# Softmax moved into the next unit's step and the last projections reordered, in a decode layer with attention and MLP on one core

## The chip, the cores and the metric

The kernel runs on one core of a Trainium2 chip. The core has a matrix engine (TensorE, PE in the profile, with its weight loads as PEld), a vector engine (VectorE, DVE), a scalar engine (ScalarE, ACT), GpSimd (POOL), and a sync engine (SP) whose queue issues nearly all transfers here. The 16 DMA engines of the core carry the transfers from device memory (HBM) to the on-chip memory. Each engine runs its own list of instructions in order and waits on semaphores for the others. The metric is the device time of one execution in microseconds; before and after are compared by the median of several executions.

## What is computed

Two branches of a transformer layer work on the same normalized input of two tokens (one per batch entry) and are added to the input: attention of 32 query heads over the last 2048 keys of a cache with 16 key heads, and an MLP with a squared ReLU.

```python
def _A_ref(x, k_cache, v_cache, wq, wo):     # B=2, D=576, Hq=32, Hkv=16, Dh=128
    W = min(4096, max(256, Sk // 4))          # Sk=8192, so W=2048
    q = (x @ wq) per head
    k, v = the last W rows of the caches, each key head used by two query heads
    scores = einsum("bhqd,bhkd->bhqk", q, k) * Dh ** -0.5
    o = einsum("bhqk,bhkd->bhqd", softmax(scores), v)
    return o @ wo
def _B_ref(x, w1, b1, w2, b2):               # F=4608
    h = x @ w1 + b1
    r = where(h > 0, h, 0)
    return (r * r) @ w2 + b2
return x + _A_ref(xn, ...) + _B_ref(xn, ...)  # xn = layernorm(x)
```

All arrays are bfloat16. With two rows of input, nearly all the bytes are caches and weights: 53.6 MB are read in one execution.

## The kernel before

The work on the caches is cut into 8 **units** (`NU`): unit `u` holds four key heads of one batch entry, 2048 KB of keys (`k_u`) and 2048 KB of values (`v_u`). Each is one transfer into a buffer of `kvpool`, which has six. The SP queue holds 25 loads in one fixed order, which runs `k0 wq k1 v0 w1 k2 v1 k3 v2 k4 v3 k5 v4 k6 v5 wo0 k7 v6 v7 wo1`, and then w2 in five pieces: `w2_0`, `w2_1`, `w2_2` (1296 KB each) and `w2_3` in two (1008 and 288 KB). A load that reuses a buffer waits in the SP queue until the last reader of that buffer is done, and the loads behind it wait too. `wo0` and `wo1` share one buffer.

One **step** (`step(u)`) does the key side of unit `u`. `transposes(u, g)`, for g = 0 to 7, turns the keys four 128x128 blocks at a time on PE into a PSUM tile `kT_ps` (three buffers), and copies the tile to SBUF, on ACT for even g and on DVE for odd g. `scores(u, w)`, for the two halves w, multiplies by the queries into `sc_ps`; each half needs the four copies of its half. In between go the value products of an earlier unit: `pv(u-2, i)`, i = 0 to 3, four matmuls each, into `pv_ps`. `pv_mix` then gathers the four parts of `pv_ps` on DVE (four instructions, three of them `mix`, the last into `acc`). `pv_out` brings one unit's `acc` to its place by a matmul into `sm`; for every fourth unit it also divides and rearranges on DVE into `ws`, which is the input of the output projection.

`softmax(u)` stands behind `scores(u, 1)`: the maximum of each row (`mx`, DVE), an offset (`m2`, shown as `m`), the maximum across partitions on GpSimd (`gmax`), two small DVE instructions (`gs`, `nb`), the exponential on ACT (`pr`, with its row sums), and a transpose on DVE (`pT`), which the value products of this unit need.

The order on PE is fixed by program order (`tc.keep_in_program_order` in `pe_mm` and `pe_tr`). On DVE and ACT only the four instructions of `pv_mix` are fixed among themselves; for the rest a scheduler of the language picks the order.

Ahead of the steps come `q_all` (query projection, which needs `wq`), and between step 1 and step 2 the hidden layer of the MLP: `mlp_h_start`, `mlp_h_all`, `mlp_h_end` (need `w1`). `mlp_h_end` copies the hidden rows to SBUF (`hrow`) and turns them into columns by 9 matmuls in fp32 with a selection matrix `sel_h`, which also adds the two partial sums (`hT_ps`).

At the end of the program stand, for unit numbers 4 to 7: step 6, the `sm` product of unit 4, all value products of unit 5, `wo_acc(0)` (32 matmuls of the first half of the output projection, into `out_ps`), the `sm` product of unit 5, step 7 without value products, the value products of units 6 and 7 with their `sm` products, `wo_acc(1)`, then `mlp_o` with `w2_0`, `w2_1` and `w2_2` (18 matmuls each, into the same `out_ps`). `out_ps` is copied to `part` by two DVE copies, `mlp_tail` multiplies with `w2_3` into `tail_ps` (28 matmuls for the first piece and 8 for the second, with the products that add `part` in between), and `fin_sb` leaves for the output.

Of the kernel before, what the change touches and what calls it, by code (L numbers as in the profile page):

```python
# [8 lines left out]
F32 = mybir.dt.float32  # L9
# [7 lines left out]
def kernel(  # L17
# [65 lines left out]
    def pe_mm(out, **kw):  # L83
        return tc.keep_in_program_order(nc.tensor.matmul(out, **kw))  # L84
# [3 lines left out]

    x2d = A_x.rearrange("b s d -> (b s) d")
# [51 lines left out]
    warm = const.tile([B, 114], F32, name="warm")  # L141
# [77 lines left out]
    sel_h = const.tile([P, NG4, B], F32, name="sel_h")  # L219
    for g in range(0, NG4, 2):  # L220
        q = (g + 2) % NG4
        idv = ident_f[:].rearrange("p (g s) -> p g s", s=32)
        nc.gpsimd.tensor_tensor(out=sel_h[:, g:g + 2, :], in0=idv[:, g:g + 2, 0:B], in1=idv[:, q:q + 2, B:2 * B],
                                op=ALU.add)
# [50 lines left out]
    def transposes(u, g):  # L275
        k_sb = k_tiles[u]
        w, gw = divmod(g, GW)
        if gw == 0:
            kT_tiles[(u, w)] = ktpool.tile([P, NT, P, 2], BF16, tag="kT_sb", name=f"kT_{u}_{w}")
        kT = kT_tiles[(u, w)]  # L280
        kT_ps = psum.tile([P, PG, P], F32, tag="kT", bufs=3, name=f"kT_ps_{u}_{g}")
        for i in range(PG):
            q = g * PG + i
            pe_tr(out=kT_ps[:, i, :], in_=k_sb[:, 2 * q * Dh:2 * (q + 1) * Dh].bitcast(F32),
                                identity=ident_f[:])
        src = kT_ps[:].rearrange("p i s -> p (i s)").bitcast(BF16)
        dst = kT[:, gw * PG:(gw + 1) * PG, :, :].rearrange("p i s e -> p (i s e)")
        if g % 2 == 0:
            nc.scalar.copy(out=dst, in_=src)  # L289
        else:  # L290
            nc.vector.tensor_copy(out=dst, in_=src)  # L291
# [16 lines left out]
    def softmax(u):  # L308
        sc_ps = sc_tiles.pop(u)[:].rearrange("p t s -> p (t s)")
        mx = work.tile([P, 1], F32, tag="mx", name=f"mx_{u}")  # L310
        nc.vector.tensor_reduce(out=mx[:], in_=sc_ps, axis=AX.X, op=ALU.max)  # L311
        m2 = work.tile([P, NC], F32, tag="m2", name=f"m2_{u}")
        nc.vector.tensor_scalar(out=m2[:], in0=offm[:], scalar1=mx[:, 0:1], scalar2=None, op0=ALU.add)  # L313
        gmax = work.tile([P, NC], F32, tag="gmax", name=f"gmax_{u}")
        nc.gpsimd.partition_all_reduce(gmax[:], m2[:], channels=P, reduce_op=ReduceOp.max)  # L315
        gs = work.tile([P, NC], F32, tag="gs", name=f"gs_{u}")
        nc.vector.tensor_tensor(out=gs[:], in0=gmax[:], in1=own_s[:], op=ALU.mult)
        nb = work.tile([P, 1], F32, tag="nb", name=f"nb_{u}")
        nc.vector.tensor_reduce(out=nb[:], in_=gs[:], axis=AX.X, op=ALU.add)  # L319
        pr = work.tile([P, NT * 32], BF16, tag="pr", name=f"pr_{u}")  # L320
        acc = keep.tile([P, Dh + 1], F32, tag="acc", bufs=4, name=f"acc_{u}")
        nc.scalar.activation(out=pr[:], in_=sc_ps, func=ACT.Exp, bias=nb[:], scale=scale, accum_out=acc[:, Dh:Dh + 1])  # L322
        pT = keep.tile([P, NT, 32], BF16, tag="pT", name=f"pT_{u}")
        nc.vector.transpose(out=pT[:].rearrange("p t m -> p (t m)"), in_=pr[:])  # L324
        pT_tiles[u], acc_tiles[u] = pT, acc
# [35 lines left out]
    def pv_out(u):  # L361
# [8 lines left out]
        if u % (2 * B) == 2 * B - 1:  # L370
            ri = work.tile([P, B], F32, tag="ri", name=f"ri_{t}")
            nc.vector.reciprocal(out=ri[:], in_=sm[:, :, Dh])
# [38 lines left out]
    def mlp_h_end():  # L411
# [10 lines left out]
        hv = hs[:].rearrange("p r (g b) -> p g r b", b=B)  # L422
        nc.vector.tensor_tensor(out=hT_sb[:].rearrange("p (g r) b -> p g r b", g=NG4), in0=hv, in1=hv, op=ALU.mult)
# [46 lines left out]
    def step(u, with_pv=True):  # L470
        with_pv = with_pv and u >= 2
        for g in range(NG):
            transposes(u, g)
            if with_pv and g == 1:
                if u >= 3:
                    pv_out(u - 3)
                pv_start(u - 2)
            if with_pv and 1 <= g <= NR:
                pv(u - 2, g - 1)
            if g == GW + 1:  # L480
                scores(u, 0)
        if with_pv:
            pv_mix(u - 2)
        scores(u, 1)
        softmax(u)
# [6 lines left out]
    softmax(0)  # L492
    load_v(2)
    step(1)
    mlp_h_start()
# [3 lines left out]
    for u in range(2, NU - 1):  # L499
        step(u)  # L500
# [69 lines left out]
```

## Time and profile before

| What | us |
|---|---|
| median of 7 runs | 138.75 |
| lowest and highest of them | 137.51, 139.52 |
| time of the profiled execution | 138.01 |
| span of the profiled execution | 136.2 |
| busy in it: PE, DVE, ACT, POOL | 95.0, 58.2, 43.8, 8.1 |

The span reaches from the first to the last instruction that the profile shows; the time of the same execution is 1.8 us longer. In the rows of the profile, "out<-in" names the tile that an instruction writes and those that it reads, and "x8" that eight of them are merged in a row. A line number such as L87 is often that of a helper: all matmuls have L84, all transposes on PE L87. A PE row's time counts a matmul to its modelled end, so that neighbouring matmuls overlap; where the time per matmul matters, the length of a merged row is divided by its count.

### The profile page before, as it was taken

To read this page: it belongs to the slowest core of one execution; us is meant where nothing else is said; L and a number is where in the kernel's file an instruction comes from. 1 tells how busy PE (TensorE), PEld (TensorE's weight loads), DVE (VectorE), ACT (ScalarE), POOL (GpSimd) and SP (SyncE) were. 2 spreads that over 40 slices of the span, in tenths; PEclk is the share of its full clock that TensorE was granted. 3 is DMA by queue.
4 is the path that set the end of the run, shared out by engine and by line. 5 is a ranking of instruction groups with operands and counts; after the bars stand their busy time and mean duration, and the time that the engine had idled before them with its cause. 6 is when DMAs were issued, how large, how long until landed. Compare 5 with 4: busy or idle time off the path is not lost.

```text
span 136.2 us, 2051 instructions
## 1 busy us (share of the span) xinstructions
PE 95.0 (70%) x839; PEld 57.7 (42%) x839; DVE 58.2 (43%) x147; ACT 43.8 (32%) x62; POOL 8.1 (6%) x28
## 2 busy tenths in 40 slices
PE   0049219779964889988778777876949884345991
PEld 0049102747731388544444434443525641112560
DVE  6914300223663000437546556566876353543021
ACT  2707300012722213351752733625522561000001
POOL 7200310001001000001001001001001001000000
PEclk9999975555797775799999999999999999855698
DMA  4999999999999999999999999999999999999500
GB/s 150 388 461 465 411 395 404 428 481 414 451 396 407 428 428 433 423 433 433 438 428 419 433 433 438 431 422 426 431 433 438 414 446 424 417 426 425 229 0 1
DMA packets 3632, 53.74 MB, mean 395 GB/s; under 512 B 412, under 2 KB 420, under 8 KB 680
## 3 DMA queue, kind: packets, MB, share of 16 engines
q1 hardware_dynamic: 3604, 53.61, 92.6%
q8 instruction: 6, 0.10, 0.3%
q10 hardware_dynamic: 20, 0.01, 0.1%
q14 instruction: 2, 0.02, 0.0%
HBM read 53.62 MB, written 0.00 MB: 394 GB/s over the span
## 4 chain that ended last, share of the span: by engine, by line
PE 42%; DMA 27%; DVE 15%; ACT 7%; issue 4%; POOL 1%; SPq 0%; POOLq 0%; ACTq 0%
PE kT_ps L87 15%; DMA w_sb<-in_B_w_dram 14%; DMA wq_sb<-in_A_wq_dram 14%; PE sc_ps L84 7%; PE out_ps L84 5%; PE pv_ps L84 5%; ACT kT L289 3%; PE hT_ps L84 3%; DVE kT L291 3%; DVE mx L311 3%; PE q_ps L84 3%; PE h_ps L84 3%; DVE mix L353 3%; ACT pr L322 2%; POOL gmax L315 1%
## 5 line engine op out<-in xcount | busy, mean ns | idle before, releaser
L87 PE MATMUL kT_ps<-ident_f,k 128*128 128x128 f32 x256 | 41.2, 308 | 4.8 <-ACT kT L289 3.4
L289 ACT COPY kT<-kT_ps 128x1024 bf16<-128x1024 bf16 x32 | 31.9, 1013 | 26.2 <-PE kT_ps L87 26.1
L87 PEld LDWEIGHTS kT_ps<-ident_f,k 128*128 128x128 f32 x256 | 32.1, 157 | 16.2 <-issue 8.7
L291 DVE COPY kT<-kT_ps 128x1024 bf16<-128x1024 bf16 x32 | 22.0, 687 | 26.2 <-PE kT_ps L87 26.2
L84 PE MATMUL sc_ps<-kT,qz 128*32 128x512 bf16 x128 | 10.5, 413 | 6.0 <-DVE kT L291 5.5
L84 PE MATMUL pv_ps<-v,pT 128*32 128x512 bf16 x128 | 12.4, 430 | 0.0
L322 ACT ACTIVATE pr<-sc_ps,nb 128x512 bf16<-128x512 f32 x8 | 5.5, 688 | 20.3 <-DVE nb L319 20.3
L84 PE MATMUL sm<-acc,tohead 128*64 128x129 f32 x16 | 4.0, 334 | 9.1 <-DVE acc L353 9.1
L315 POOL PARTITION_ALL_REDUCE gmax<-m x8 | 3.0, 369 | 94.1 <-DVE m L313 94.1
L324 DVE STREAM_TRANSPOSE pT<-pr 128x512 bf16<-128x512 bf16 x8 | 5.7, 711 | 6.3 <-ACT pr L322 6.3
L84 PEld LDWEIGHTS <-xnT 128*4 128x4 bf16 x90 | 3.0, 117 | 12.2 <-issue 11.9
L84 PE MATMUL q_ps<-wq_sb,xnT 128*4 128x512 bf16 x36 | 4.0, 628 | 5.3 <-DMA wq_sb<-in_A_wq_dram 5.3
L311 DVE TENSOR_REDUCE mx<-sc_ps 128x1 f32<-128x512 f32 x8 | 5.5, 692 | 4.2 <-PE sc_ps L84 3.8
L84 PE MATMUL out_ps<-wo,ws 128*2 128x288 bf16 x64 | 6.0, 359 | 1.5 <-DVE ws L382 1.5
L84 PEld LDWEIGHTS sm<-acc,tohead 128*64 128x64 f32 x16 | 1.7, 152 | 12.2 <-DVE acc L353 9.7
L84 PEld LDWEIGHTS <-qz 128*32 128x32 bf16 x128 | 2.1, 98 | 10.3 <-DVE kT L291 7.1
L538 ACT CAST fin_sb<-tail_ps 2x144 bf16<-2x144 f32 x2 | 0.5, 272 | 17.5 <-PE tail_ps L84 17.5
L84 PE MATMUL h_ps<-w_sb,xnT 128*4 128x384 bf16 x54 | 4.2, 478 | 2.3 <-DMA w_sb<-in_B_w_dram 2.3
L353 DVE SCALAR_TENSOR_TENSOR mix<-pv_ps,own_j,mix 128x128 f32<-128x128 f32 x16 | 5.6, 348 | 0.4
L84 PEld LDWEIGHTS <-pT 128*32 128x32 bf16 x128 | 3.3, 98 | 5.4 <-issue 4.8
L87 PE MATMUL pro_ps<-ident,xs 2*128 2x2 bf16 x10 | 0.6, 164 | 7.0 <-DVE xs L179 7.0
L84 PE MATMUL hT_ps<-sel_h,hrow 100*128 100x8 f32 x18 | 4.5, 386 | 1.1 <-ACT hrow L414 1.1
(77 smaller groups left out, 65.7 us busy)
## 6 DMA issues: line engine op xcount, KB each, us to landing
k<-in_A_k_cache_dram SPq DMA_DIRECT2D x8, 2048.0 KB, 8.2
v<-in_A_v_cache_dram SPq DMA_DIRECT2D x8, 2048.0 KB, 13.4
w_sb<-in_B_w_dram SPq DMA_DIRECT2D x1, 5184.0 KB, 18.8
wq_sb<-in_A_wq_dram SPq DMA_DIRECT2D x1, 4608.0 KB
wo<-in_A_wo_dram SPq DMA_DIRECT2D x2, 2304.0 KB
w<-in_B_w_dram SPq DMA_DIRECT2D x3, 1296.0 KB, 13.6
w<-in_B_w_dram SPq DMA_DIRECT2D x1, 1008.0 KB
w<-in_B_w_dram SPq DMA_DIRECT2D x1, 288.0 KB
```

The lines of the kernel that those rows point to most:

```text
L84: return tc.keep_in_program_order(nc.tensor.matmul(out, **kw))
L87: return tc.keep_in_program_order(nc.tensor.transpose(**kw))
L289: nc.scalar.copy(out=dst, in_=src)
L291: nc.vector.tensor_copy(out=dst, in_=src)
L311: nc.vector.tensor_reduce(out=mx[:], in_=sc_ps, axis=AX.X, op=ALU.max)
L315: nc.gpsimd.partition_all_reduce(gmax[:], m2[:], channels=P, reduce_op=ReduceOp.max)
L322: nc.scalar.activation(out=pr[:], in_=sc_ps, func=ACT.Exp, bias=nb[:], scale=scale, accum_out=acc[:, Dh:Dh + 1])
L324: nc.vector.transpose(out=pT[:].rearrange("p t m -> p (t m)"), in_=pr[:])
L353: op = nc.vector.scalar_tensor_tensor(out=nx, in0=pv_ps[:, j, :], scalar=own_j[:, j:j + 1], in1=acc, op0=ALU.mult, op1=ALU.add)
L538: cp(out=fin_sb[:, q * OQ:(q + 1) * OQ], in_=mlp["out"][32 * k:32 * k + B, :])
```

## The change

Four things are changed, and the DMA list on SP stays as it was in its order.

**The steps.** `softmax(u)` is cut into three functions, `softmax_max` (mx, m2, gmax), `softmax_exp` (gs, nb, pr) and `softmax_tr` (pT). They are issued inside step u+1, behind its first, second and fourth group of transposes. The value products of unit `p` are issued in two halves: parts 0 and 1 behind the third and fourth group, parts 2 and 3 and `pv_mix` behind the last. The `sm` product (`pv_out(o)`) comes behind the fourth group. Step 2 has no value products any more: those of unit 0 are issued as a whole between step 1 and the MLP, those of unit 1 in step 3, and so on to those of unit 5 in step 7.

**The order on DVE and ACT.** The copies of the transposes and all instructions of the softmax are put under `tc.keep_in_program_order` (`pin`).

**The hidden layer of the MLP.** The 9 fp32 matmuls with `sel_h` become 9 transposes on PE in two groups (5 and 4). ACT copies the one partial sum out of PSUM (`hodd`), DVE adds it to the other in two instructions a group, and one DVE instruction does ReLU and square. `sel_h` and its two GpSimd additions go away.

**The end.** `wo_acc(0)` comes right behind step 6, step 7 takes the value products of unit 5 and the `sm` product of unit 4 into it, the softmax of unit 7 is put between the value products of unit 6 and what follows them, and `mlp_o` with `w2_0` comes ahead of `wo_acc(1)`.

```diff
+    def pin(ins):
+        return tc.keep_in_program_order(ins)
...
-            nc.vector.tensor_copy(out=dst, in_=src)
+            pin(nc.vector.tensor_copy(out=dst, in_=src))
...
-        hT_ps = psum.tile([P, FR, NG4 * B], F32, tag="sc", bufs=2, name="hT_ps")
-        for r in range(FR):
-            pe_mm(hT_ps[:, r, :], lhsT=hrow[:, r:HW:FR], rhs=sel_h[0:RB, :, :].rearrange("p g b -> p (g b)"),
-                  start=True, stop=True)
-        hs = const.tile([P, FR, NG4 * B], F32, name="hs")
-        nc.scalar.activation(out=hs[:], in_=hT_ps[:], func=ACT.Relu)
+        hs = const.tile([P, NG4 * FR, B], F32, name="hs")
+        for r0, n in ((0, 5), (5, FR - 5)):
+            ps = psum.tile([P, 5, RB], F32, tag="sc", bufs=2, name=f"hT_ps_{r0}")
+            for r in range(n):
+                pe_tr(out=ps[:, r, :], in_=hrow[:, r0 + r:HW:FR], identity=ident_f[0:RB, 0:RB])
+            a = ps[:, 0:n, 0:B]
+            even, odd = [bass.AP(a.tensor, a.offset + s, [a.ap[0], a.ap[1], [32, NG4], a.ap[2]]) for s in (0, B)]
+            od = work.tile([P, 5, NG4, B], F32, tag="hodd", name=f"hodd_{r0}")
+            nc.scalar.copy(out=od[:, 0:n, :, :], in_=odd)
+            for g in range(0, NG4, 2):
+                q = (g + 2) % NG4
+                nc.vector.tensor_tensor(out=hs[:].rearrange("p (g r) b -> p r g b", g=NG4)[:, r0:r0 + n, g:g + 2, :],
+                                        in0=even[:, :, g:g + 2, :], in1=od[:, 0:n, q:q + 2, :], op=ALU.add)
...
-    def step(u, with_pv=True):
...
+    def step(u, p=None, o=None):
+        if p is not None:
+            pv_start(p)
+        transposes(u, 0)
+        softmax_max(u - 1)
+        transposes(u, 1)
+        softmax_exp(u - 1)
+        transposes(u, 2)
+        if p is not None:
+            pv(p, 0)
+        transposes(u, 3)
+        if p is not None:
+            pv(p, 1)
+        softmax_tr(u - 1)
+        if o is not None:
+            pv_out(o)
+        transposes(u, 4)
+        scores(u, 0)
+        for g in range(GW + 1, NG):
             transposes(u, g)
...
+        for i in range(2, NR):
+            if p is not None:
+                pv(p, i)
+        if p is not None:
+            pv_mix(p)
         scores(u, 1)
-        softmax(u)
...
     step(1)
+    pv_all(0)
     mlp_h_start()
...
-        step(u)
+        step(u, u - 2 if u > 2 else None, u - 3 if u > 2 else None)
...
-    pv_out(NU - 4)
-    pv_all(NU - 3)
     wo_acc(0)
+    step(NU - 1, NU - 3, NU - 4)
+    pv_start(NU - 2)
+    for i in range(NR):
+        pv(NU - 2, i)
+    softmax_max(NU - 1)
     pv_out(NU - 3)
-    step(NU - 1, with_pv=False)
-    pv_all(NU - 2)
+    softmax_exp(NU - 1)
+    pv_mix(NU - 2)
+    softmax_tr(NU - 1)
     pv_out(NU - 2)
     pv_all(NU - 1)
     pv_out(NU - 1)
+    mlp_o(*W2P[0])
     wo_acc(1)
-    for w in W2P[:NG4 - 1]:
+    for w in W2P[1:NG4 - 1]:
         mlp_o(*w)
```

What this does to the order is seen on DVE, around the end of a step's scores. Before, on DVE from the third copy of unit 4's keys on (`kT_ps_5` is group 5; `mx_812` and `pT_825` belong to the softmax of the same unit, the mixes to the value products of unit 2):

```order
L291 COPY kT_1_758<-kT_ps_5_769 128x1024
L291 COPY kT_1_758<-kT_ps_7_791 128x1024
L350 TENSOR_SCALAR mix_0_797<-pv_ps_733,own_j 128x128
L353 SCALAR_TENSOR_TENSOR mix_1_799<-pv_ps_733,own_j,mix_0_797 128x128
L311 TENSOR_REDUCE mx_812<-sc_ps_775 128x1
L353 SCALAR_TENSOR_TENSOR mix_2_801<-pv_ps_733,own_j,mix_1_799 128x128
L313 TENSOR_SCALAR m_4_814<-offm,mx_812 128x8
L353 SCALAR_TENSOR_TENSOR acc_596<-pv_ps_733,own_j,mix_2_801 128x128
L317 TENSOR_TENSOR gs_818<-gmax_816,own_s 128x8
L319 TENSOR_REDUCE nb_820<-gs_818 128x1
L324 STREAM_TRANSPOSE pT_825<-pr_822 128x512
L291 COPY kT_0_833<-kT_ps_1_840 128x1024
```

The same place on DVE now (`mx_831` is the maximum of the scores just made):

```order
L288 COPY kT_1_759<-kT_ps_7_788 128x1024
L357 TENSOR_SCALAR mix_0_802<-pv_ps_709,own_j 128x128
L360 SCALAR_TENSOR_TENSOR mix_1_804<-pv_ps_709,own_j,mix_0_802 128x128
L360 SCALAR_TENSOR_TENSOR mix_2_806<-pv_ps_709,own_j,mix_1_804 128x128
L360 SCALAR_TENSOR_TENSOR acc_621<-pv_ps_709,own_j,mix_2_806 128x128
L310 TENSOR_REDUCE mx_831<-sc_ps_766 128x1
L312 TENSOR_SCALAR m_4_833<-offm,mx_831 128x8
L288 COPY kT_0_824<-kT_ps_1_837 128x1024
L320 TENSOR_TENSOR gs_843<-gmax_835,own_s 128x8
L322 TENSOR_REDUCE nb_845<-gs_843 128x1
L288 COPY kT_0_824<-kT_ps_3_860 128x1024
L331 STREAM_TRANSPOSE pT_870<-pr_847 128x512
```

The first two DVE copies of the next unit's keys (`kT_ps_1`, `kT_ps_3`) now stand inside the softmax chain, and all four mixes stand ahead of the maximum.

The other place is PE at the end of the program, behind the last value product. Before (`wo_1060` is the second half of the output projection's weights):

```order
L84 LDWEIGHTS pT_1211
L84 MATMUL pv_ps_1238<-v_943,pT_1211 32x512
L84 MATMUL sm_1071<-acc_1209,tohead 64x129
L84 LDWEIGHTS ws_1268
L84 MATMUL out_ps<-wo_1060,ws_1268 2x288
```

And now (`w_0_1052` is `w2_0`):

```order
L84 LDWEIGHTS pT_1240
L84 MATMUL pv_ps_1243<-v_933,pT_1240 32x512
L84 MATMUL sm_1142<-acc_1231,tohead 64x129
L84 LDWEIGHTS hT_sb
L84 MATMUL out_ps<-w_0_1052,hT_sb 2x288
```

The 18 products with `w2_0` now stand between the last `sm` product and the 32 products with `wo1`, which wait for `ws`.

More of the change, by code (lines that the diff above doesn't have):

```diff
@@ L140 @@
     nc.vector.memset(eps_t[:], 1e-5)
-    warm = const.tile([B, 114], F32, name="warm")
+    warm = const.tile([B, 122], F32, name="warm")
     nc.scalar.activation(out=warm[:, 0:1], in_=eps_t[:], func=ACT.Sqrt)
@@ L218 @@
             nc.gpsimd.tensor_copy(out=sel_q[:, k, :, h, :], in_=ident_f[:].rearrange("p (g s) -> p s g", s=32)[:, a:a + B, :])
[L219 to L224, printed above, removed]
     sel4 = const.tile([NG4, P], BF16, name="sel4")
@@ L288, in transposes @@
         if g % 2 == 0:
-            nc.scalar.copy(out=dst, in_=src)
+            pin(nc.scalar.copy(out=dst, in_=src))
         else:
-            nc.vector.tensor_copy(out=dst, in_=src)
+            pin(nc.vector.tensor_copy(out=dst, in_=src))
     def scores(u, w):
@@ L371, in pv_out @@
             ri = work.tile([P, B], F32, tag="ri", name=f"ri_{t}")
-            nc.vector.reciprocal(out=ri[:], in_=sm[:, :, Dh])
+            pin(nc.vector.reciprocal(out=ri[:], in_=sm[:, :, Dh]))
             od = work.tile([P, B, DW, WR], F32, tag="od", bufs=1, name=f"od_{t}")
@@ L491 @@
         scores(0, w)
-    softmax(0)
     load_v(2)
     step(1)
+    pv_all(0)
     mlp_h_start()
```

36 lines of the change are left out of this document (15 added, 21 removed).

## Prediction

> **What bounds the kernel now.** I read the stretches of the span first (start and end, length, busy time of PE, PEld, DVE, ACT and POOL, granted clock, DMA share, GB/s).
>
> ```profile
> 2.30:127.00 124.70, 88.81 (x731) 54.03 (x733) 55.34 (x138) 43.29 (x60) 6.28 (x21) 0.85 1.00 426
> 127.00:128.00 1.00, 1.00 (x12) 0.56 (x10) 0.00 (x0) 0.00 (x0) 0.00 (x0) 0.50 0.69 274
> 128.00:129.00 1.00, 1.00 (x18) 0.64 (x16) 0.00 (x0) 0.00 (x0) 0.00 (x0) 0.92 0.31 122
> ```
>
> The DMA engines are full (share 1.00, 426 GB/s) to 127 and done near 129. No order of compute can bring the bytes earlier; it can only shorten what is left behind them, some 7 us of the span. So I need to know when each piece lands. The SP queue's timeline (start, length) and the page's sizes, with the median time from issue to landing where it is known:
>
> ```profile
> 87.49 2.99 SPq L103 DMA_DIRECT2D v<-in_A_v_cache_dram  x2
> 105.84 0.33 SPq L115 DMA_DIRECT2D wo<-in_A_wo_dram  x1
> 106.22 3.33 SPq L128 DMA_DIRECT2D w<-in_B_w_dram  x5
> ...
> k<-in_A_k_cache_dram SPq DMA_DIRECT2D x8, 2048.0 KB, 8.2
> v<-in_A_v_cache_dram SPq DMA_DIRECT2D x8, 2048.0 KB, 13.4
> ...
> wo<-in_A_wo_dram SPq DMA_DIRECT2D x2, 2304.0 KB
> w<-in_B_w_dram SPq DMA_DIRECT2D x3, 1296.0 KB, 13.6
> w<-in_B_w_dram SPq DMA_DIRECT2D x1, 1008.0 KB
> w<-in_B_w_dram SPq DMA_DIRECT2D x1, 288.0 KB
> ```
>
> I take the 13.6 to be w2_0's: 106.2 + 13.6 = 119.8. At 426 GB/s, 1296 KB take 3.1 us, 1008 KB 2.4, 288 KB 0.7, 2304 KB 5.5 and 2048 KB 4.9. Forward from 119.8: w2_1 lands at 122.9, w2_2 at 126.0, w2_3 at 128.4 and 129.1, which is where the DMA share ends, so the reading holds. Backward: wo1 116.7, v7 111.2, v6 106.3, k7 101.4, wo0 96.5, k6 86.0, and one unit every 9.8 us before that.
>
> Now the chain that ended last, in order of time (start, length, what):
>
> ```profile
> 71.35 0.64 PE sc_ps L84 x8
> ...
> 81.02 0.65 PE sc_ps L84 x6
> ...
> 106.56 0.60 PE kT_ps L87 x4
> ...
> 112.55 0.65 PE sc_ps L84 x7
> 113.21 0.70 DVE mx L311
> ...
> 115.20 0.79 ACT pr L322 x2
> 116.01 0.71 DVE pT L324
> ...
> 118.86 1.85 PE pv_ps L84 x16
> ...
> 123.94 0.59 DVE ws L382
> 124.57 6.87 PE out_ps L84 x81
> ...
> 132.76 0.74 PE tail_ps L84 x12
> ```
>
> Two things are to be seen. Step 7 starts at 106.56, though its keys have been there since 101.4. And from 113.20 to 124.53 a chain of softmax, value products, mixes and `ws` runs with PE mostly waiting, while wo1 and w2_0 land; only then does PE start on all 32 + 54 projection matmuls at once. The bound of the end is this compute chain, 4.4 us later than the last byte would ask (133.50 against 129.1).
>
> **The change, part by part.**
>
> *The step.* Before, from one unit's scores to the next (71.35 to 81.02) it is 9.67 us. The stretch of just that step:
>
> ```profile
> 71.35:81.02 9.67, 7.69 (x67) 4.32 (x67) 5.64 (x14) 4.62 (x6) 0.37 (x1) 1.00 1.01 430
> ```
>
> PE is the busiest with 7.69, so the new step lies between 7.7 (all softmax hidden) and, if nothing were hidden, 9.67. A third figure: step 7 of before has no value products and no exposed softmax, and takes 106.56 to 113.20, 6.6 us; with 1.85 us of value products at most, 8.5. I take 8.5, nearest to that row. All three are under the 9.8 us in which a unit lands. So the steps catch up with the stream and then wait for keys, and the saving of some 1.2 us a step is worth nothing in itself: DMA covers it. Loads keep their order; each waits for a buffer that a step frees, and steps come no later, so the stream stays full; wo1 waits for `wo_acc(0)`, now near 98.6 instead of 105.8, with v6 and v7 still ahead of it. Cost and gain on the path: 0.
>
> *The MLP's hidden layer.* Rows of the timeline for this and the next parts (start, length, instruction, in brackets the idle time ahead of it and what ended it):
>
> ```profile
> 48.17 4.46 PE L84 MATMUL hT_ps<-sel_h,hrow 100*128 100x8 f32 x18 [1.06 <-ACT hrow L414]
> ...
> 54.92 1.12 PE L87 MATMUL kT_ps<-ident_f,k 128*128 128x128 f32 x4
> ...
> 103.67 2.13 PE L84 MATMUL out_ps<-wo,ws 128*2 128x288 bf16 x32
> ...
> 124.57 3.86 PE L84 MATMUL out_ps<-wo,ws 128*2 128x288 bf16 x32 [1.52 <-DVE ws L382]
> ...
> 131.47 0.72 PE L84 MATMUL tail_ps<-w,hT_sb 128*2 128x144 bf16 x24
> 131.78 0.93 DVE L527 COPY part<-out_ps 2x288 f32<-2x288 f32 x2 [7.26 <-PE out_ps L84]
> ```
>
> The 9 matmuls run as 18 passes of 0.25 us. Nine transposes cost between 9 x 0.25 = 2.2 us and as much as now, 4.5; with a wait between the groups for one ACT copy and two DVE adds (under 1 us) it is 3.2 to 5.5 in place of 4.46, and I take 3.2, the pass count being halved. The value products of unit 0 go into PE's wait for w1. Either end moves step 2 by about 1 us, which the steps' slack against the stream covers (if it didn't, step 7 would be later by that).
>
> *wo_acc(0) and step 7.* Step 6 has its keys at 86.0 and ends by 95.7 at the longest; `wo_acc(0)` then needs wo0 at 96.5 and takes 2.1 us (103.67) to 3.9 us (124.57, at half clock), to 98.6 or 100.4; step 7 waits for k7 at 101.4. With 8.5 us its scores end at 109.9 instead of 113.20. Without the catching up (step 3 starting as before at 71.99 - 9.67 = 62.3, five steps of 9.67 and 2.1 for `wo_acc(0)`) it would be 112.8.
>
> *From there to ws.* Before, 11.33 us. Now the four mixes of unit 6 stand ahead of pT: pr ends 2.8 us behind the scores as before (113.20 to 116.01), the mixes fill the time to about 3.4, pT takes 0.7, the value products 1.85, and from their end (120.71) to ws (124.53) it is 3.8 as before. Sum 9.8, so ws stands at 119.7.
>
> *The last projections.* PE starts `mlp_o` with w2_0 at 119.8: 18 matmuls at half clock, 3.86 / 32 = 0.12 each, to 122.0. ws is there before; with scores that end at 112.8 it would come 0.6 late. `wo_acc(1)` follows without a gap. The clock decides the rest:
>
> ```profile
> 42.00:43.00 1.00, 0.14 (x4) 0.10 (x7) 0.27 (x1) 0.70 (x2) 0.00 (x0) 0.91 0.96 410
> 43.00:44.00 1.00, 1.00 (x16) 0.42 (x12) 0.44 (x1) 0.00 (x0) 0.00 (x0) 0.50 0.95 410
> ...
> 114.00:118.00 4.00, 0.03 (x4) 0.00 (x0) 2.39 (x8) 0.78 (x2) 0.36 (x1) 0.99 0.99 421
> ...
> 124.80:128.10 3.30, 3.30 (x30) 1.78 (x28) 0.00 (x0) 0.00 (x0) 0.00 (x0) 0.50 0.87 358
> 128.20:132.00 3.80, 3.80 (x86) 2.77 (x82) 0.22 (x1) 0.00 (x0) 0.00 (x0) 1.00 0.06 22
> ```
>
> Before, PE began at 124.57 at half clock and got full clock at about 128.2, 3.6 us later. I bound the same here from 3.6 to 7 us, so 123.4 to 126.8. At full clock a matmul takes 2.13 / 32 = 0.067. With the early end, 30 of the 68 up to w2_1 are done at 123.4, the other 38 by 126.0, and the last 18 with w2_2 by 127.2. With the late end 58 are done at 126.8 and the other 28 by 128.7. The `part` copies (0.93) end at 128.1 or 129.6. The first w2_3 piece lands at 128.4; its 28 matmuls take 0.72 x 28 / 24 = 0.84, to 129.2; the `part` products and the last 8 take 0.4 and 0.74, to 130.4 (the second piece is in at 129.1). Before this was 133.50, so **3.1 us less**; the late clock costs up to 0.4 of it.
>
> The sum: 138.01 - 3.1 = 134.9 for the profiled execution. The median is 0.74 above that execution. If that difference comes from the transfers it stays (135.6), if from the compute chain it goes; I take the middle, **135.3**.
>
> [...] In the rows above PE stood still from 114 to 118 and had half clock behind it; at 42 to 43 a shorter stop (PE busy 0.14 of that us) was enough. [...] What that would cost is the first rival.
>
> **Rivals.** *Step 7 at half clock throughout.* For it: the wait from 98.6 to 101.4. A group of transposes then takes 1.12 (54.92) in place of 0.6, eight of them 4.2 more, with scores and value products about 5, so scores at 114.9 and ws at 124.7. PE stops at 122.0, starts cold at 124.7: 30 matmuls at 0.12, 38 at 0.067, then 0.93 and 1.14, which ends at 132.9, a gain of 0.6: 137.4. Half of the step cold puts ws at 122.2 and costs little. I put the case, with those of part of the loss, between 136.2 and 137.8. Against it: busy PE got its clock back within 3.6 us.
>
> *The last projections stay at half clock.* 86 matmuls at 0.12 from 119.8 end at 130.1; 28 tail matmuls at twice 0.84 at 131.8, the rest at twice 1.14 at 134.1: 138.6, no change. For it: 118 to 128 ran at 0.50. Against it: unbroken work of the same kind ended that.
>
> *The pinned order makes the step longer* (slower). DVE now holds two key copies behind mx and behind gs, which waits for GpSimd, and all four mixes ahead of mx; if DVE's order set the pace, with two more mixes (0.7) and pT (0.7) ahead of copies that PE waits for, a step would take 9.67 + 1.4 = 11.1. From 62.3, five such steps and 2.1 for `wo_acc(0)` put the last scores at 119.9, ws at 129.7, and the end 3.6 + 2.5 + 0.93 + 1.14 behind at 137.9: 4.4 later, 142.4. It decides from a step of about 10.2 on, where the end stands as before. Against it: DVE is busy 5.64 of 9.67.
>
> **How the numbers follow.** Forecast 0.68, step 7 cold 0.14, projections cold 0.11, longer step 0.07. The range runs from 134.2 (the forecast's 134.9 less the 0.5 by which the fastest run shown lies under the profiled one, rounded out) to 137.9, which leaves out the last two cases, 0.18. About 1% (1.4 us) is what a measurement of this kernel can tell from no change. Faster by more: the forecast and 0.10 of the cold step, 0.78. Within it: 0.04 of the cold step and the cold projections, 0.15. Slower: 0.07.
>
> **What would show it.** DMA share full to 127 again; each step's first transpose released by a key load and not by ACT; step 7 starting near 101.4 and its scores ending near 110; PE on w2_0 near 119.8 with no stop between it and wo1; full clock before 126.8; the first tail matmul released by w2_3's load. It is wrong if the stream has gaps, if ws comes behind 122, or if PE is still on `out_ps` past 129.

## The result and the profile after

| | before | after |
|---|---|---|
| median, us | 139.09 (31 runs) | 134.22 (12 runs) |
| lowest and highest, us | 137.51, 141.36 | 133.99, 134.43 |
| profiled execution: time, span, us | 138.01, 136.2 | 134.18, 132.4 |

The ratio after/before is 0.968, with a 95% interval of 0.965 to 0.971: the kernel is 3.2% faster. A ratio is formed only from those executions that lie within 1.5% of the fastest of their kernel, so it isn't the quotient of the two medians. The executions of before lie 3.85 us apart, those of after 0.44.

The page of after, the granted clock, the DMA share and the group of the key transposes:

```profile
PEclk9999985555599999599999958999967999755698
DMA  4999989999998999999999999999999999999950
...
L87 PE MATMUL kT_ps<-ident_f,k 128*128 128x128 f32 x256 | 40.0, 311 | 7.4 <-DMA k<-in_A_k_cache_dram 6.9
```

The transfers are as full as before, and now they are what PE waits for: of the 7.4 us that PE stands still ahead of transposes, 6.9 end with a key load. The chain that ended last, in order of time (start, length, what), says the same:

```profile
38.55 28.18 DMA k<-in_A_k_cache_dram
...
66.87 1.50 PE kT_ps L87 x12
...
74.19 27.14 DMA k<-in_A_k_cache_dram
...
101.47 1.50 PE kT_ps L87 x12
...
107.92 20.43 DMA w<-in_B_w_dram
128.38 1.29 PE tail_ps L84 x44
```

Key loads carry it to 101.47, the last w2 load to 128.38, and 1.29 us of matmuls are left. In before the chain ran through scores, softmax and `ws`, and ended at 132.76 + 0.74 = 133.50; now it ends at 129.67, which is 3.83 less, and the two profiled executions are 3.83 apart as well. The whole gain is in where compute stands behind the stream at the end.

PE's timeline in after from the early part to the end (start, length, instructions; in brackets the idle time ahead and what ended it):

```profile
46.22 0.82 PE L87 MATMUL hT_ps<-ident_f,hrow 100*128 100x100 f32 x5 [1.06 <-ACT hrow L421]
47.71 0.67 PE L87 MATMUL hT_ps<-ident_f,hrow 100*128 100x100 f32 x4 [0.67 <-DVE hs L433]
48.22 1.48 PE L87 MATMUL kT_ps<-ident_f,k 128*128 128x128 f32 x12
...
57.87 1.53 PE L87 MATMUL kT_ps<-ident_f,k 128*128 128x128 f32 x12
...
96.56 3.40 PE L84 MATMUL out_ps<-wo,ws 128*2 128x288 bf16 x32 [2.84 <-DMA wo<-in_A_wo_dram]
101.47 1.50 PE L87 MATMUL kT_ps<-ident_f,k 128*128 128x128 f32 x12 [1.51 <-DMA k<-in_A_k_cache_dram]
...
108.29 0.62 PE L84 MATMUL sc_ps<-kT,qz 128*32 128x512 bf16 x8 [0.24 <-DVE kT L288]
...
119.67 2.32 PE L84 MATMUL out_ps<-w,hT_sb 128*2 128x288 bf16 x18 [2.55 <-DMA w<-in_B_w_dram]
```

`wo_acc(0)`, step 7 and the `w2_0` products each begin when their bytes land, and so does the tail at 128.38. And one thing the prediction hadn't counted on: step 3 starts at 57.87, against 62.44 before. Nearly all of the lag behind the stream was gone before the steps that were to make it up.

### The profile page after: what moved, and what is told of

Same layout as the page of the kernel before. It is cut to its first block, busy times and chain, and to the rows that moved or that the text cites. A ratio compares the mean times of both kernels' runs of the same rounds, so it can differ in the third digit from the quotient of the medians.

```text
span 132.4 us, 2040 instructions
## 1 busy us (share of the span) xinstructions
PE 90.1 (68%) x830; PEld 55.5 (42%) x830; DVE 59.6 (45%) x151; ACT 43.8 (33%) x63; POOL 7.7 (6%) x26
## 4 chain that ended last, share of the span: by engine, by line
DMA 71%; PE 21%; DVE 2%; ACT 2%; issue 1%; SPq 1%; DVEq 0%; ACTq 0%
DMA k<-in_A_k_cache_dram 42%; DMA w<-in_B_w_dram 15%; DMA wq_sb<-in_A_wq_dram 14%; PE kT_ps L87 9%; PE sc_ps L84 4%; PE q_ps L84 3%; PE qs_ps L84 3%; DVE kT L288 1%; PE pv_ps L84 1%; PE tail_ps L84 1%; ACT kT L286 1%; ACT pr L325 1%; PE sm L84 1%; DVE qrow L252 1%; SPq L106 0%
## 5 line engine op out<-in xcount | busy, mean ns | idle before, releaser
L87 PE MATMUL kT_ps<-ident_f,k 128*128 128x128 f32 x256 | 40.0, 311 | 7.4 <-DMA k<-in_A_k_cache_dram 6.9
L87 PEld LDWEIGHTS kT_ps<-ident_f,k 128*128 128x128 f32 x256 | 33.1, 160 | 16.7 <-issue 12.2
L84 PE MATMUL sc_ps<-kT,qz 128*32 128x512 bf16 x128 | 10.8, 424 | 4.3 <-DVE kT L288 2.8
L84 PE MATMUL pv_ps<-v,pT 128*32 128x512 bf16 x128 | 10.6, 396 | 1.0 <-DVE acc L360 0.8
L84 PE MATMUL out_ps<-wo,ws 128*2 128x288 bf16 x64 | 6.9, 396 | 2.8 <-DMA wo<-in_A_wo_dram 2.8
L84 PE MATMUL out_ps<-w,hT_sb 128*2 128x288 bf16 x54 | 4.7, 337 | 2.6 <-DMA w<-in_B_w_dram 2.6
L84 PEld LDWEIGHTS <-ws 128*2 128x2 bf16 x64 | 3.8, 114 | 5.9 <-issue 3.2
L84 PEld LDWEIGHTS <-hT_sb 128*2 128x2 bf16 x90 | 3.1, 89 | 5.8 <-issue 3.1
L84 PEld LDWEIGHTS <-pT 128*32 128x32 bf16 x128 | 2.7, 94 | 5.3 <-issue 2.7
```

What stands on the lines that cost most here:

```text
L87: return tc.keep_in_program_order(nc.tensor.transpose(**kw))
```

## The experiments

Each kernel was measured beside the kernel before on the same chip; ratios are to that one. Letters in the quoted expectations stand for theories, A among them for the account on record (short steps catch up, and the order at the end brings `ws` in time).

**1. The end alone.** Before, with `wo_acc(0)` right behind step 6 and the `w2_0` products ahead of `wo_acc(1)`; step, softmax and hidden layer as before.

```diff
+    wo_acc(0)
     pv_out(NU - 4)
     pv_all(NU - 3)
-    wo_acc(0)
     pv_out(NU - 3)
...
+    mlp_o(*W2P[0])
     wo_acc(1)
-    for w in W2P[:NG4 - 1]:
+    for w in W2P[1:NG4 - 1]:
```

> The kernel before with the new order of the projections alone: wo_acc(0) right behind step 6 and the w2_0 products ahead of wo_acc(1); softmax, steps and hidden layer as before. Theory A (the stream sets the end, and compute counts only where ws comes behind about 122 us): the last scores stay near 113.2 and ws near 124.5, so PE still starts late; only the 18 products with w2_0 move into the wait, and the time is 137 to 138 (1.2 to 2 us less than before). Rival B (each part saves its own time on a compute chain): the same 1.2 to 2 us. Rival C (the order at the end brings nothing by itself): 139.1.

Median 137.39 (136.75 to 138.35, 10 runs) against 139.35; ratio 0.992, interval 0.988 to 0.996. The new order is worth something as long as `ws` is late: PE has the `w2_0` products to do in place of the 1.52 us that it waited for `ws` before. But it doesn't bring `ws` forward (in its profiled execution PE starts on `w2_0` at 124.78), and most of the gain is missing.

**2. The softmax back to its place.** After, with the three parts of the softmax issued together behind their own step's scores; the order on VectorE and ScalarE is still fixed as written.

```diff
         transposes(u, 0)
-        softmax_max(u - 1)
         transposes(u, 1)
-        softmax_exp(u - 1)
...
-        softmax_tr(u - 1)
...
         scores(u, 1)
+        softmax_max(u)
+        softmax_exp(u)
+        softmax_tr(u)
```

> The changed kernel with the softmax of a unit put back behind its own scores; all else as changed. Theory A: the steps take 9.7 to 10.4 us again, but start near 57 and end near 98, so step 7 still starts near 101.4, and ws comes near 121 to 122.5: 134.2 to 134.8. Rival B: the exposed softmax is paid in each step again, 4 to 5 steps of 1.5 to 2.3 us: 140 or more; at least 139 if the moved softmax is the source of the gain.

The four executions took 134.21, 134.25, 138.64 and 139.18: two like after, two like before. The ratio, formed from the two near 134.2, is 0.971 (0.964 to 0.977): in those two the old place of the softmax cost nothing, so the gain doesn't hang on moving it. The profiled one is the 138.64, and no trace of the faster two was kept. PE's timeline of the 138.64, ahead of the fourth group of transposes of two neighbouring steps:

```profile
70.61 0.66 PE L87 MATMUL kT_ps<-ident_f,k 128*128 128x128 f32 x4 [1.83 <-ACT kT L286]
...
83.99 0.66 PE L87 MATMUL kT_ps<-ident_f,k 128*128 128x128 f32 x4 [3.17 <-ACT kT L286]
```

The two are 13.4 us apart, where the stream gives 9.8. With a fixed order and a softmax in one piece, the key copies queue behind the softmax on ACT and DVE, and PE waits 1.83 and 3.17 us in these two steps. A stretch of the same execution (start and end, length, busy PE, PEld, DVE, ACT, POOL, granted clock, DMA share, GB/s):

```profile
66.00:80.00 14.00, 11.47 (x84) 6.89 (x77) 6.81 (x17) 4.62 (x6) 0.36 (x1) 0.76 1.00 428
```

The mean clock was 0.76 there, so the wait and the clock are mixed up in it, and this trace doesn't show which of them made the execution long. Experiment 6 fills the wait with work.

**3. The second output projection ahead of w2 again.** After, with `wo_acc(1)` before the `w2_0` products again.

```diff
-    mlp_o(*W2P[0])
     wo_acc(1)
-    for w in W2P[1:NG4 - 1]:
+    for w in W2P[:NG4 - 1]:
```

> The changed kernel with wo_acc(1) ahead of the w2_0 products, as before. Theory A: ws is ready at 118.6 and wo1 at 116.6, so PE takes the 32 products from 118.6, w2_0's at about 122, and is done with w2_2 at the same time: 134.2, within 0.3. Rival B: the 18 products moved ahead are paid again, 1.2 to 2.2 us: 135.4 to 136.4.

Median 134.51 (134.17 to 134.90, 4 runs), ratio 0.973 (0.968 to 0.978): the median is 0.3 us above after's, and the ranges overlap. With `ws` in time the order of these products costs next to nothing.

**4. The value products of unit 5 ahead of `wo_acc(0)` again.**

```diff
+    pv_out(NU - 4)
+    pv_all(NU - 3)
     wo_acc(0)
-    step(NU - 1, NU - 3, NU - 4)
+    step(NU - 1)
```

> The changed kernel with the value products of unit 5 and the sm product of unit 4 ahead of wo_acc(0) and out of step 7, as before; softmax moved as changed. Theory A: all of this lies ahead of k7's landing at 101.3 (step 6 ends at 93.7 and PE waits from there), so nothing changes: 134.2, within 0.3. Rival B: value products, mixes and sm product of unit 5 stand alone again, 2 to 3 us: 136 to 137.

Median 134.23 (134.11 to 134.35, 4 runs), ratio 0.971 (0.967 to 0.975): no loss. Moving them into step 7 was not needed either.

**5. The order on VectorE and ScalarE left to the scheduler.** After, with

```diff
     def pin(ins):
-        return tc.keep_in_program_order(ins)
+        return ins
```

> The changed kernel without the fixed order on DVE and ACT (the pin function leaves the instruction free); PE's order as changed. The scheduler then puts the whole softmax of a unit ahead of the next unit's key copies on DVE and ACT again. Theory A with the clock (an exposed softmax leaves PE idle about 1.8 us a step; where that takes the clock to half, steps take 12 to 13 us, fall behind the stream and put ws behind 122): executions from 134.2 to 139, spread by 2 us or more, median 135 to 138. Rival D (the order of issue on PE is enough, the fixed order does nothing): 134.2 with a spread under 0.5.

Median 134.26 (134.16 to 134.47, 6 runs), ratio 0.970 (0.965 to 0.975). The wide spread that I had expected did not come. PE's timeline shows why:

```profile
67.04 1.50 PE L87 MATMUL kT_ps<-ident_f,k 128*128 128x128 f32 x12 [2.61 <-DMA k<-in_A_k_cache_dram]
...
73.87 0.62 PE L84 MATMUL sc_ps<-kT,qz 128*32 128x512 bf16 x8 [0.24 <-DVE kT L288]
76.58 1.50 PE L87 MATMUL kT_ps<-ident_f,k 128*128 128x128 f32 x12 [2.09 <-DMA k<-in_A_k_cache_dram]
```

From the keys' landing to the end of the scores it takes 7.5 us (67.04 to 74.49), and DVE does the first part of the softmax (`mx` to `nb`, 74.54 to 76.55) in the 2.09 us in which PE waits for the next keys; the exponential (from 76.65 on ACT) and `pT` follow while PE turns the first of them. Nothing has to be fixed for that.

**6. The wait of experiment 2 filled with work.** Experiment 2, with ten matmuls of 32x256 in each step behind the first value product part. They write to partitions of `out_ps` (made 128 partitions high for it) that nobody reads, and add no result.

```diff
+    def keep_busy(n):
+        for _ in range(n):
+            pe_mm(out_ps[64:96, 0:256], lhsT=ident[:, 0:32], rhs=par[:].rearrange("p e a i -> p (e a i)"),
+                  start=True, stop=True, skip_group_check=True, tile_position=(0, 64))
...
             pv(p, 0)
+        keep_busy(10)
         transposes(u, 3)
```

> The kernel with the softmax put back behind its own scores, plus ten matmuls a step (32 x 256, into unused partitions of out_ps, read by nobody) at the place where PE waits for the ACT copy, about 1.1 us at full clock. Clock theory: the bunched softmax costs only because PE's wait takes the clock to half; with the wait filled the clock stays at 1.0 through the steps and every execution takes 134.2 to 134.8, spread under 0.7. Rival E (the bunched chain itself makes the late steps, the clock only follows): executions still between 134 and 139, or all later by the 5 to 6 us of added matmuls.

Median 135.69 (134.33 to 135.97, 6 runs), ratio 0.977 (0.971 to 0.984). The same stretch of its profiled execution (135.79):

```profile
66.00:80.00 14.00, 12.04 (x119) 7.57 (x111) 8.91 (x22) 5.12 (x7) 0.73 (x2) 1.00 1.01 432
```

With more work on PE the clock stayed at 1.00 in that stretch, and none of these six executions came near 139. That fits the clock, falling in the wait, as what made the long ones, but six executions against four don't show it. The steps of this profile take 10.0 to 10.4 us (the added matmuls of one end at 70.17, and PE still waits 1.49 us for a key copy on ACT), and yet step 7 is released by its keys:

```profile
77.22 24.30 DMA k<-in_A_k_cache_dram
101.66 2.28 PE kT_ps L87 x12
...
104.48 1.71 PE out_ps L84 x10
```

So the 1.5 us that the median lies above after's are not the price of longer steps. In this execution `ws` stands at 123.75, where after has 118.58. Of these 5.2 us, 2.7 arise in step 7, which takes 10.1 us (101.66 to 111.79) in place of 7.4: the ten added matmuls stand in its chain, and its first 12 transposes take 2.28 in place of 1.50, at a mean clock of 0.88 over 93 to 107. The other 2.3 arise behind its scores, where the mixes of unit 6 now stand behind `pT` and the last value products take 1.90 us in place of 1.21. The added work and the order are thus mixed in the 1.5 us; the two executions of 134.2 in experiment 2, with the same order and without the added work, say that the order need not cost anything.

**7 and 8. More work in each step.** After, with 8 (then 24) more transposes in each of the steps 3 to 6, into a tile that nobody reads.

```diff
+        if u in (3, 4, 5, 6):
+            for m in range(2):
+                x_ps = psum.tile([P, PG, P], F32, tag="kT", bufs=3, name=f"x_ps_{u}_{m}")
+                for i in range(PG):
+                    pe_tr(out=x_ps[:, i, :], in_=k_tiles[u][:, 2 * i * Dh:2 * (i + 1) * Dh].bitcast(F32),
+                          identity=ident_f[:])
```

> The changed kernel with 8 more transposes (1.2 us of PE, into kT_ps buffers that nobody reads) in each of steps 3 to 6. Theory A: steps go from about 7.2 to 8.4 us, under the 9.8 in which a unit lands: 134.2, within 0.3. Rival B (steps on the chain): 4 x 1.2 more, 139.

> The same with 24 more transposes, 3.5 us, in each of steps 3 to 6. Theory A: steps of 10.7 to 11 us from k3's landing at 57 end at 100 to 101, wo_acc(0) at 102.5 to 104, step 7 starts 1.5 to 2.5 us later than k7 lands, its scores end at 110.5 to 111.5 and ws comes at 120 to 121.5, still under 122: 134.2 to 134.8 though 14 us of work were added. Rival B: 148.

Medians 134.28 (134.23 to 134.73, 4 runs) and 134.36 (134.32 to 134.40, 4 runs), ratios 0.970 for both (0.965 to 0.976). The chain of the kernel with 24 of them:

```profile
71.82 0.62 PE sc_ps L84 x8
...
82.59 0.62 PE sc_ps L84 x8
...
93.37 0.62 PE sc_ps L84 x8
...
99.46 1.97 PE out_ps L84 x32
101.52 1.50 PE kT_ps L87 x12
```

Its steps take 10.8 us (71.82 to 82.59 to 93.37), a whole us more than the stream and 1.1 more than the steps of before, and still step 7 starts at 101.52. PE comes to `wo_acc(0)` at 99.46, 3 us after wo0 has landed, and is done with it just when k7 is there. I had expected it 1.5 to 2.5 us behind k7's landing; the steps ended earlier than forecast (99.46, not 100 to 101). So the length of the step isn't what was won: steps longer than before's give the same time, if they start without a lag.

**9, 10 and 11. The early part by itself.** What is left is all that stands ahead of step 3. Three kernels were made from before, with its steps, its softmax and its end. In the first, `pv_all(0)` comes ahead of the MLP and step 2 has no value products:

```diff
     def step(u, with_pv=True):
-        with_pv = with_pv and u >= 2
+        with_pv = with_pv and u >= 3
...
     step(1)
+    pv_all(0)
     mlp_h_start()
```

In the second only the hidden layer is as in after (nine transposes, a copy and additions; the lines are in the diff of the change):

```diff
-        for r in range(FR):
-            pe_mm(hT_ps[:, r, :], lhsT=hrow[:, r:HW:FR], rhs=sel_h[0:RB, :, :].rearrange("p g b -> p (g b)"),
-                  start=True, stop=True)
...
+            for r in range(n):
+                pe_tr(out=ps[:, r, :], in_=hrow[:, r0 + r:HW:FR], identity=ident_f[0:RB, 0:RB])
...
```

The third has both edits. L in these expectations is the theory that the lag with which step 3 begins decides.

> The kernel before with one edit: the value products of unit 0 go as a whole ahead of the MLP's hidden layer, into PE's wait for w1, and out of step 2. Softmax, order on DVE and ACT, hidden layer and end as before. Theory L (the steps of before keep pace with the stream but never make up the 5 us that step 3 starts behind k3; what takes away this early lag brings the gain): step 3 starts 2 to 3 us earlier, step 7 at about 103.8, ws at about 121.8: 135 to 136.5. Rival S (the moved softmax and the new order at the end bring it): 138.5 to 139.1.

> The kernel before with one edit: the hidden layer's 9 fp32 products with sel_h as 9 transposes, as in the changed kernel. Theory L: 2 us of the lag go, step 7 at 104.3 to 104.6, ws at 122.3 to 122.6: 135.8 to 137. Rival S: 138.5 to 139.1.

> Both of these edits on the kernel before; softmax, fixed order and the order at the end as before. Theory L: step 3 starts with k3 at about 57.5, four steps of 9.67 end at 96.5, value products of unit 5 and wo_acc(0) at 102, ws at 120: the whole gain, 134.2 to 134.7. Rival S: 138 to 139, at most the sum of the two single edits' gains with ws still behind 122.

| kernel | median (range, runs) | ratio, interval |
|---|---|---|
| unit 0's value products early | 137.42 (136.82 to 139.17, 4) | 0.989, 0.982 to 0.996 |
| hidden layer alone | 134.30 (134.09 to 134.66, 4) | 0.963, 0.959 to 0.967 |
| both | 134.26 (134.16 to 134.29, 4) | 0.962, 0.958 to 0.966 |

The hidden layer alone brings all of it, more than either theory gave it (135.8 us at best). PE's timeline of that kernel:

```profile
42.57 4.48 PE L84 MATMUL h_ps<-w_sb,xnT 128*4 128x384 bf16 x54 [4.70 <-DMA w_sb<-in_B_w_dram]
48.12 1.28 PE L87 MATMUL hT_ps<-ident_f,hrow 100*128 100x100 f32 x9 [1.07 <-ACT hrow L408]
49.24 1.04 PE L87 MATMUL kT_ps<-ident_f,k 128*128 128x128 f32 x8
...
57.37 1.09 PE L87 MATMUL kT_ps<-ident_f,k 128*128 128x128 f32 x8
...
102.63 1.53 PE L87 MATMUL kT_ps<-ident_f,k 128*128 128x128 f32 x12
...
120.45 4.00 PE L84 MATMUL out_ps<-wo,ws 128*2 128x288 bf16 x32 [1.52 <-DVE ws L376]
...
128.36 0.61 PE L84 MATMUL tail_ps<-w,hT_sb 128*2 128x144 bf16 x28 [0.30 <-DMA w<-in_B_w_dram]
```

The rows of before for the same places:

```profile
52.49 1.95 PE L87 MATMUL kT_ps<-ident_f,k 128*128 128x128 f32 x8
...
62.44 1.09 PE L87 MATMUL kT_ps<-ident_f,k 128*128 128x128 f32 x8
...
106.49 1.53 PE L87 MATMUL kT_ps<-ident_f,k 128*128 128x128 f32 x12
```

Step 2 starts 3.25 us earlier (52.49 to 49.24), nearly all of it the transposes' 1.28 in place of 4.46. Then step 2 itself is 1.8 shorter (52.49 to 62.44 is 9.95, 49.24 to 57.37 is 8.13). The stretches tell why; first before, then the hidden layer alone:

```profile
48.20:52.50 4.30, 4.30 (x19) 4.30 (x19) 0.00 (x0) 0.00 (x0) 0.00 (x0) 0.67 1.01 427
52.50:62.30 9.80, 9.02 (x68) 5.21 (x68) 3.61 (x7) 4.28 (x5) 0.00 (x0) 0.80 1.00 430
```

```profile
48.10:49.40 1.30, 1.28 (x11) 1.28 (x12) 0.20 (x2) 0.19 (x1) 0.00 (x0) 1.00 0.93 391
49.40:57.30 7.90, 7.12 (x68) 3.98 (x65) 3.96 (x11) 4.23 (x5) 0.00 (x0) 1.00 1.00 429
```

Step 2 runs at 1.00 instead of 0.80. Together step 3 starts 5.07 us earlier, which is the whole lag: in the kernel with both edits PE waits for the keys of unit 3 and starts on them at 57.21.

```profile
57.21 1.13 PE L87 MATMUL kT_ps<-ident_f,k 128*128 128x128 f32 x8 [0.95 <-DMA k<-in_A_k_cache_dram]
```

The expectation of 2 us had counted the shorter transposes and not what the clock did to step 2. The steps of the kernel with the hidden layer alone are then 9.67 us long, as in before, and of the 5.07 us 3.86 are left at step 7 (106.49 to 102.63). The rest goes ahead of `wo_acc(0)` and in it, which takes 2.93 in place of 2.13 at a clock of 0.79.

With unit 0's value products moved alone, the chain shows that the old matmuls still take 4.46; about half of the lag stays, and `ws` comes at 122.14 + 0.59, a us later than expected (of the 2.52 us that step 3 starts earlier, 1.36 are left at step 7, behind value products of unit 5 that take 1.78 and a `wo_acc(0)` of 3.13, which in before take 1.05 and 2.13):

```profile
47.20 4.46 PE hT_ps L84 x18
...
122.14 0.59 DVE ws L382
122.77 7.49 PE out_ps L84 x81
```

In after itself the lag went in another way. The products with w1, first after, then before:

```profile
42.55 2.60 PE L84 MATMUL h_ps<-w_sb,xnT 128*4 128x384 bf16 x54 [1.18 <-DMA w_sb<-in_B_w_dram]
42.86 4.25 PE L84 MATMUL h_ps<-w_sb,xnT 128*4 128x384 bf16 x54 [2.31 <-DMA w_sb<-in_B_w_dram]
```

With unit 0's value products in the wait for w1, that wait is 1.18 us in place of 2.31, and the 54 products run at full clock (1.00 over 43.00 to 45.10, where before had 0.50 over 42.84 to 46.23), as they do in experiment 9 (2.60 there too, 1.00 over 43.50 to 45.90). So the hidden layer's turn starts 1.95 us earlier (46.22, 48.17), takes 2.32 less up to step 2 (48.22, 52.49), and step 2 is 0.30 shorter: 4.57 in all. In after about half of the lag thus went with the hidden layer's new form and most of the rest with the products of w1; experiment 10 shows that the hidden layer is enough by itself.

Four kernels in one table, by their profiled executions (the end is that of the last PE piece in the chain that ended last):

| kernel | step 3 starts | step 7 starts | `ws` ready | end | time |
|---|---|---|---|---|---|
| before | 62.44 | 106.49 | 124.53 | 133.50 | 138.01 |
| unit 0's products early | 59.92 | 105.13 | 122.73 | 132.32 | 136.82 |
| hidden layer alone | 57.37 | 102.63 | 120.4 | 129.82 | 134.33 |
| after | 57.87 | 101.47 | 118.58 | 129.67 | 134.18 |

From the third row to the fourth `ws` comes 1.8 us earlier and the end only 0.15: by then the last w2 load decides.

**12. The last load cut in another place.** After, with the last group of w2 in pieces of 6 and 3 columns of blocks in place of 7 and 2.

```diff
-    W2P = [(0, 0, 9), (1, 0, 9), (2, 0, 9), (3, 0, 7), (3, 7, 9)]
+    W2P = [(0, 0, 9), (1, 0, 9), (2, 0, 9), (3, 0, 6), (3, 6, 9)]
```

> The changed kernel with the last weights cut at row group 6 instead of 7 (1008 + 288 KB become 864 + 432 KB), to start the tail products earlier. Theory A: the first piece lands 0.35 us earlier, 24 instead of 28 products stand behind it, and the last 12 instead of 8 behind the last byte at 129.0: PE ends 0.1 to 0.25 us earlier, 134.0 to 134.1. Rival: the last landing alone counts and the four more products behind it cost 0.1 us: 134.3.

Median 134.14 (133.96 to 134.50, 6 runs), ratio 0.962 (0.959 to 0.965). That is 0.08 under after's median and inside its spread: whether it is better stays open. With compute in time there is little left behind the last byte.

## Why the prediction was right, and where it was not

The time was forecast at 135.3, in a range of 134.2 to 137.9, and came at 134.22; that it would be faster was right. That the time lies in the range is luck: it is 0.02 above the lower bound, and the forecast was a us too high. What happens at the end was right (step 7 on time, `ws` in time for w2, the tail behind the last load); what brings step 7 there on time was not.

- *The stream.* Right. Landing times were forecast from sizes and rate: wo0 96.5, k7 101.4, w2_0 119.8, w2_3 128.4. PE was released by them at 96.56, 101.47, 119.67 and 128.38.
- *The steps.* Forecast 8.5 us long, they take 7.5 (step 3 from 57.87 to 65.3; step 5, at half clock over 76.75 to 80.15, 9.0), and steps 4 to 7 each wait for their keys. The 8.5 held 1.85 us for the value products, from a row of before at a clock of 0.50 (117.93 to 128.15); at 1.00 the 16 take 1.05 (from 102.80 in before). That "the steps catch up with the stream" is the step that failed: there was nothing to catch up. Against k3's landing at 57.2 (when PE is released by it in experiment 11) step 3 began 0.7 late in after, 5.2 late in before. Longer steps (10.8 us) give the same time, and before's own steps of 9.67 do too.
- *The hidden layer.* This is the term that was mis-sized, and the reason for the failed step. It was put at 3.2 us in place of 4.46, "about 1 us, which the steps' slack against the stream covers (if it didn't, step 7 would be later by that)". Nine transposes take 1.28 (experiment 10), not 9 x 0.25, and step 2 runs at 1.00 behind them, where before had a mean of 0.80. And before has no slack to cover it: from the start of step 3 to that of step 7 the stream takes 44.2 us (k3 at 57.2, k7 at 101.4), before's compute 44.05 (62.44 to 106.49). For the old steps the remark in the brackets is what held: step 7 came 3.86 us earlier, and the median fell from 139.68 to 134.30 with this edit alone. Whether the slack of the new steps would have covered it was not measured. Both 9.67 and 9.8 stood in the prediction; I used them to say that the new steps catch up, and didn't ask how the old ones had fallen behind, nor whether they would ever make it up.
- *`wo_acc(0)` and step 7.* The times were right (96.56 to 99.96, step 7 at 101.47, scores to 108.9 for a forecast 109.9). The moves were not needed (experiment 4).
- *From the scores to `ws`.* Forecast 9.8 us, measured 9.7 (108.9 to 118.58), but by terms that cancel: `pT` ended 4.6 us behind the scores and not 4.1, as `mx` now starts 0.66 behind them, after the four mixes of unit 5, and the value products took 1.21 and not 1.85.
- *The last projections.* Half clock was forecast until some time between 123.4 and 126.8. The 3.6 us of the early bound were read from before; the 7 of the late one were my estimate, which no run shows. In after half clock lasted 4.86 us from PE's start on `w2_0` (119.67 to 124.53). Stretches of after:

```profile
121.00:124.00 3.00, 3.00 (x30) 1.63 (x26) 0.00 (x0) 0.00 (x0) 0.00 (x0) 0.50 1.00 424
124.00:128.00 4.00, 3.46 (x52) 2.15 (x48) 0.48 (x2) 0.00 (x0) 0.00 (x0) 0.93 0.87 361
```

  The clock came back at 124.53, within the bounds, and the projections were done before the last load. The order of `w2_0` ahead of wo1 was to keep PE from waiting for `ws`; it is worth 0.3 us at most where `ws` is in time (experiment 3) and 0.8% where it is late (experiment 1).
- *The tail.* Forecast 0.84 + 0.4 + 0.74 = 1.98 behind the first piece of w2_3, measured 1.29. The old rows were taken from a place where these matmuls alternate with others and the `part` products wait for a DVE copy; in after the copies were done at 128.42, ahead of them. This is the 0.7 us by which the profiled execution (134.18) lies under the forecast of 134.9.
- *The median.* Half of 0.74 was added, as I couldn't say whether before's spread comes from transfers or compute. After's median lies 0.04 from its profiled execution and its range is 0.44 us: the stream hardly varies, and so the spread of before was most likely that of its compute chain (the kernels of experiments 10 and 11, made from before, spread by 0.57 and 0.13). Why that chain varies was not shown.
- *The rivals.* That step 7 would keep full clock was an estimate. It did:

```profile
76.60:79.30 2.70, 2.70 (x16) 2.37 (x16) 0.76 (x2) 1.01 (x1) 0.00 (x0) 0.53 1.03 443
96.60:99.90 3.30, 3.30 (x32) 1.70 (x31) 0.00 (x0) 0.00 (x0) 0.00 (x0) 0.59 1.03 442
101.50:110.00 8.50, 7.46 (x75) 4.39 (x79) 5.28 (x12) 4.67 (x6) 0.00 (x0) 1.00 1.02 433
```

  But the first two rows show that the clock did dip, behind waits of 2.30 and 2.84 us for a load. Behind others of 1.52 and 1.51 us it was 1.00 (66.87 to 69.00, 101.47 to 104.00). The dips cost about 1.2 us each (2.67 in place of 1.50 for the 12 transposes at 76.60, 3.40 in place of 2.13 for `wo_acc(0)`) and fell where there was slack. The pinned order didn't make the step longer in after. With the softmax in one piece steps of 10.0 to 10.4 us were seen at full clock (experiment 6), about the 10.2 from which the third rival would decide; but they started without a lag, and step 7 still began on its keys.

What stays open: whether the shorter steps alone, with the old early part, would also catch up, as the prediction had it. That kernel wasn't run. By its arithmetic (7.5 against 9.8) they would; the runs show only that in after they didn't have to.

## What to carry to other kernels

Where compute runs beside a stream at nearly the same pace, note for each stage how late it starts against the landing of its data, and go back to the stage where the lag arose: with 9.67 us of work per 9.8 us of transfers a delay of 5 us early in the program was still there at the end, and removing it there gave the same time as all four changes together. An edit may be costed at nothing only where that slack has been added up, over all the steps that remain, and is larger than the edit. And when several edits go in together, run each one on the old kernel alone: taking single edits back from the new one (experiments 3 to 5) showed only that none of those three was needed, not which one did it.

## What the runs showed of the hardware

- *The 9 fp32 matmuls with `sel_h` took 0.248 us a pass, and the clock fell while they ran.* They run as 18 passes with 8 moving columns, 4.46 us in before and again 4.46 in experiment 9, where the projection ahead of them had run at 1.00; the transposes of the same blocks take 0.14 each (nine in 1.28, experiment 10). In before the clock fell at 49.65, while they ran (1.00 over 48.17 to 49.64, 0.50 over 49.66 to 52.49), though PE was busy in all of the 4.30 us at 48.20 to 52.50, and step 2 began at 0.50 (a mean of 0.80 over it). In experiment 9, with PE busy throughout, the mean clock was 0.72 over 47.20 to 51.60 and 0.56 over 51.70 to 56.50. With a wait of the same length ahead (1.07 us, 1.06 in before) and the nine transposes in place of the matmuls (experiment 10), the clock was 1.00 over them and over step 2; in after, where they come in two groups with waits, it fell once, to 0.50 from 52.85 to 56.26.
- *The clock rose in before while PE did nothing but fp32 transposes.* PE did scores to 31.8 and then only fp32 transposes of 128x128, 24 of them, to 36.6; the clock was 0.50 when they began and 1.00 from 36.00 on:

```profile
31.00:36.00 5.00, 5.00 (x32) 4.20 (x21) 2.33 (x6) 2.35 (x3) 0.40 (x1) 0.50 1.02 440
36.00:37.00 1.00, 1.00 (x11) 0.60 (x13) 0.43 (x2) 1.00 (x3) 0.00 (x0) 1.00 0.86 373
```

- *The clock had two values, 1.00 and 0.50, and the distances between its changes were multiples of 3.41 us.* In before it changed at 18.93, 36.00, 42.83, 46.24, 49.65, 56.48, 117.92 and 128.16 us by the clock record of the trace: the distances are 17.07, 6.83, 3.41, 3.41, 6.83, 61.44 and 10.24, each within 0.1 of a multiple of the shortest. In after it was 0.50 from 18.72 to 35.79, 52.85 to 56.26, 76.74 to 80.16, 97.22 to 100.64 and 114.29 to 124.53, for 17.07, 3.41, 3.41, 3.41 and 10.24 us. Two waits in after (74.30 to 76.60, 93.72 to 96.56) were each followed by one of the stretches of 3.41, two of 1.5 us (65.35 to 66.87, 99.96 to 101.47) by a clock of 1.00; in experiment 5 the 12 transposes behind waits of 2.61 and 2.09 us took 1.50, as at 1.00 in after. What makes the clock fall or rise, and how much work or waiting that takes, no run here shows.
